# Outputs of two chunks in one transfer of 4 KB rows, in place of one transfer each of 2 KB rows

## The chip, the core and the metric

One core of a Trainium2 chip. The metric is the time of one execution in microseconds on the device. An execution's time is some 1.8 us above the span that its profile shows from the first to the last instruction.

## The reference

Thresholded attention over 8 batches, 8 heads, 576 positions and head size 64, followed by a gated MLP with a mixing over positions. Cut to its shapes and steps:

```python
scores = 0.125 * q @ k.T                     # 8 x 8 x 576 x 576
scores = where(scores >= max - tau, scores, -1e9)
attn   = softmax(scores);  x = attn @ v      # then x as 8 x 576 x 512
h      = relu(x @ w_in)                      # 1024 wide, halves u and v
v_n    = layernorm(v)
v_s    = w_spatial @ v_n + b_spatial         # over the 576 positions
out    = (u * v_s) @ w_out                   # 8 x 576 x 512, float32
```

## The kernel before

The program is one list of 144 steps, some 3 us each. In every step TensorE makes a block of scores, VectorE takes the maximum, ScalarE exponentiates, VectorE (in some steps ScalarE) masks; the probabilities `p` are then transposed by a DMA into `pT`, which TensorE multiplies with `v`. The MLP of a batch is woven in between the attention steps of the next batch and a half: 18 steps make a batch's period. The output of a batch is made in four chunks of 128 rows (`moe_o`, two steps apart) and a remainder of 64 rows. Transfers go out on the queue of SyncE, the engine that here only issues them, in program order, from a list `sends` that each step empties after its transpose.

```python
orr = ctx.enter_context(tc.tile_pool(name="orr", bufs=3))
ptp = ctx.enter_context(tc.tile_pool(name="ptp", bufs=5))      # pT
...
def moe_o(b, c):                       # chunk c of batch b
    def mm():
        t = hold["t"] = bank()         # 4 matmuls into PSUM
        ...
    def ev():
        o = orr.tile([P, 512], F32, name="o") if not wide else stage()
        (nc.scalar.copy if not wide or c % 2 == 0 else nc.vector.tensor_copy)(
            out=o[:n], in_=hold["t"][:n])
        dst = (out[b, 0:512, :].rearrange("(p c) n -> p c n", c=4)[:, c, :] if c < 4
               else out[b, 512:576, :])
        sends.append(lambda: nc.sync.dma_start(out=dst, in_=o[:n]))
...
def mask():                            # the step before's probabilities
    ...
    if c % 2:
        dst = pts[i, c // 2] = ptp.tile([P, 2, 9, P], BF16, name="pT")
        nc.sync.dma_start_transpose(out=dst.rearrange("p c b s -> p (c b) s"),
                                    in_=pt.rearrange("p c s -> p (c s)"))
...
def step(i, c, fs):
    ...
    ready = sends[:]                   # queued by this step and the one before
    sends.clear()
    if unmasked:
        mask()
    for f in ready:
        f()
```

`wide` is empty in the steady part and filled in the tail. Each partition of a chunk holds one row of 2 KB of the output; four chunks of one partition lie side by side in memory, which is why two chunks make rows of 4 KB.

Of the kernel before, what the change touches and what calls it, by code (L numbers as in the profile page):

```python
# [8 lines left out]
F32 = mybir.dt.float32  # L9
# [8 lines left out]
def kernel(  # L18
# [17 lines left out]
    nc = tc.nc  # L36
# [6 lines left out]
    P = 128  # L43
# [7 lines left out]
    xtp = ctx.enter_context(tc.tile_pool(name="xtp", bufs=2))  # L51
    mw = ctx.enter_context(tc.tile_pool(name="mw", bufs=2))
    vr = ctx.enter_context(tc.tile_pool(name="vr", bufs=4))
    orr = ctx.enter_context(tc.tile_pool(name="orr", bufs=3))
    sqr = ctx.enter_context(tc.tile_pool(name="sqr", bufs=1))
    inner = ctx.enter_context(ExitStack())
    ps_f = ctx.enter_context(tc.tile_pool(name="ps_f", bufs=2, space=PSUM))
# [40 lines left out]
    sends = []  # L98
# [118 lines left out]
    wide = []  # L217
    turn = [0]

    def bank(dtype=F32, n=512):  # L220
        if wide:

            turn[0] += 1
            if turn[0] % 8 not in (2, 3):
                return wide[0].tile([P, n], dtype, name="t")
        return ps_f.tile([P, n], dtype, name="f")
# [183 lines left out]
        return "act", mm, ev  # L410

    us, gs = {}, {}
    later = []

    def ends(t, b):
# [112 lines left out]
    def moe_o(b, c):  # L528
        hold = {}
        n = P if c < 4 else 64  # L530

        def mm():
            t = hold["t"] = bank()
            for f in range(4):
                nc.tensor.matmul(out=t[:n], lhsT=gs[b][:, f, c * P:c * P + n],  # L535
                                 rhs=w_o[:, f, :], start=(f == 0), stop=(f == 3))

        def ev():
            o = orr.tile([P, 512], F32, name="o") if not wide else stage()
            (nc.scalar.copy if not wide or c % 2 == 0 else nc.vector.tensor_copy)(  # L540
                out=o[:n], in_=hold["t"][:n])
# [3 lines that stand above are left out]
        return "act", mm, ev  # L545
# [99 lines left out]
    def stage():  # L645

        t = ld_ring[len(staged) // 3 % 2][len(staged) % 3]
        half = len(staged) // 6 % 2
        staged.append(t)
        return t.rearrange("p h c d -> p (h c d)")[:, 512 * half:512 * half + 512]  # L650
# [120 lines left out]
    for b in range(B):  # L771
        n = dict.fromkeys("vuso", 0)
# [132 lines left out]
```

## Time and profile before

| | us |
|---|---|
| median of 3 runs (480.43 to 480.60) | 480.46 |
| the profiled execution | 482.52 |
| its span | 480.7 |

The prediction shows what bounds the kernel. Two more answers belong to it. The first is the view of the tile `o` (line, engine, operation, count: shortest, median and longest in ns, first and last start in us): twenty copies on ScalarE, one for each output that the change touches.

```profile
L540 ACT COPY o<-f x20: 566/585/595, 171.0 to 411.6; 128x512 f32<-128x512 f32 x20
```

The second is the view of who waited for whom (us in total, times, longest): all that TensorE ever waits for a transpose, one place, seen once by the weight load and once by the matmul.

```profile
PEld L289 <- DMA pT<-p: 2.0, 1, 2.0
PE f L289 <- DMA pT<-p: 1.7, 1, 1.7
```

### The profile page before, as it was taken

To read this page: it belongs to the slowest core of one execution; us is meant where nothing else is said; L and a number is where in the kernel's file an instruction comes from. 1 tells how busy PE (TensorE), PEld (TensorE's weight loads), DVE (VectorE), ACT (ScalarE), POOL (GpSimd) and SP (SyncE) were. 2 spreads that over 40 slices of the span, in tenths; PEclk is the share of its full clock that TensorE was granted. 3 is DMA by queue.
4 is the path that set the end of the run, shared out by engine and by line. 5 is a ranking of instruction groups with operands and counts; after the bars stand their busy time and mean duration, and the time that the engine had idled before them with its cause. 6 is when DMAs were issued, how large, how long until landed. Compare 5 with 4: busy or idle time off the path is not lost.

```text
span 480.7 us, 9934 instructions
## 1 busy us (share of the span) xinstructions
PE 449.2 (93%) x3691; PEld 237.4 (49%) x3691; DVE 410.9 (85%) x563; ACT 390.8 (81%) x677; POOL 226.2 (47%) x403
## 2 busy tenths in 40 slices
PE   7788888889999999899999999999999999999995
PEld 4344444444545545354554545445554545445542
DVE  4989888989989997989889888899889998898573
ACT  4789999999879797878978898798978889797251
POOL 3453334794438543555328642375436743253021
PEclk9899999999999999999999999999999999999999
DMA  7979899979988999998989999987998989677523
GB/s 212 265 156 212 184 228 207 188 162 196 187 185 196 168 213 206 179 187 191 199 188 217 177 205 197 217 173 161 212 199 191 207 173 208 144 114 112 149 92 106
DMA packets 227568, 88.49 MB, mean 184 GB/s; under 512 B 197056, under 2 KB 221760, under 8 KB 227520
## 3 DMA queue, kind: packets, MB, share of 16 engines
q1 hardware_dynamic: 226864, 86.98, 86.4%
q8 instruction: 29, 0.48, 0.4%
q0 software_dynamic: 160, 0.52, 0.3%
q10 hardware_dynamic: 496, 0.36, 0.2%
q14 instruction: 19, 0.16, 0.1%
HBM read 33.31 MB, written 9.44 MB: 89 GB/s over the span
## 4 chain that ended last, share of the span: by engine, by line
PE 50%; DVE 20%; ACT 19%; issue 7%; DMA 2%; POOL 0%; POOLq 0%; ACTq 0%
PE s L563 16%; DVE negm L604 9%; DVE p L585 7%; PE s L566 6%; ACT e L621 5%; ACT e L627 5%; PE f L294 4%; PE f L476 4%; PE f L245 3%; PE f L506 2%; PE f L535 2%; ACT vrel L444 2%; PE f L289 2%; DMA pT<-p 2%; ACT p L623 1%
## 5 line engine op out<-in xcount | busy, mean ns | idle before, releaser
L604 DVE TENSOR_REDUCE negm<-s 128x2 f32<-128x1152 f32 x144 | 194.9, 1353 | 35.5 <-PE s L566 35.0
L563 PE MATMUL s<-qkT 64*128 64x512 f32 (+1 forms) x640 | 162.9, 639 | 14.3 <-ACT e L627 8.0
L585 DVE SCALAR_TENSOR_TENSOR p<-e,ctau 128x1152 bf16<-128x1152 f32 x91 | 132.9, 1461 | 1.2 <-ACT e L627 1.1
L627 ACT ACTIVATE e<-s,negm 128x576 f32<-128x576 f32 x182 | 124.7, 740 | 7.8 <-DVE negm L604 7.1
L566 PEld LDWEIGHTS s<-kd,qkT 128*128 128x128 f32 (+1 forms) x320 | 41.5, 178 | 110.7 <-issue 100.1
L621 ACT ACTIVATE e<-s,negm 128x576 f32<-128x576 f32 x106 | 72.8, 740 | 16.9 <-DVE negm L608 11.7
L268 POOL COPY kd<-qkT 64x64 f32<-64x64 f32 x62 | 27.0, 435 | 101.3 <-ACT qkT L263 99.5
L566 PE MATMUL s<-kd,qkT 128*128 128x128 f32 (+1 forms) x320 | 69.9, 322 | 0.0
L563 PEld LDWEIGHTS s<-qkT 64*128 64x128 f32 (+1 forms) x640 | 42.1, 174 | 45.8 <-ACT e L627 17.2
L452 POOL TENSOR_SCALAR nmean<-sm 128x1 f32<-128x1 f32 (+1 forms) x35 | 16.5, 472 | 68.1 <-ACT vrel L444 63.0
L294 PEld LDWEIGHTS <-pT 128*128 128x128 bf16 x1024 | 41.8, 97 | 8.7 <-issue 5.4
L294 PE MATMUL f<-v,pT 128*128 128x65 bf16 x992 | 44.9, 194 | 0.0
L623 ACT ACTIVATE p<-e 128x1152 bf16<-128x1152 f32 x37 | 43.0, 1163 | 1.2
L136 POOL COPY qn<-ql 128x640 f32<-128x640 f32 x31 | 35.0, 1129 | 15.0 <-DMA ql<-in_k_dram 11.0
L289 PE MATMUL f<-v,pT 128*128 128x130 bf16 x124 | 27.2, 219 | 4.7 <-DMA pT<-p 1.7
L464 POOL TENSOR_SCALAR vn<-vrel,rs,nm 128x512 bf16<-128x512 f32 (+1 forms) x34 | 29.6, 872 | 3.7
L506 PE MATMUL f<-wsT,vn 128*128 128x512 bf16 x125 | 31.0, 379 | 0.0
L476 PE MATMUL f<-xT,w_in 128*128 128x512 bf16 x112 | 28.6, 379 | 0.8 <-DVE xn L303 0.7
L434 PE MATMUL f<-w_in,xT 128*128 128x512 bf16 x112 | 28.7, 379 | 0.0
L252 ACT COPY qkT<-f 128x512 f32<-128x512 f32 x31 | 18.2, 588 | 12.8 <-PE f L245 12.8
L303 DVE TENSOR_TENSOR xn<-f,r 128x256 bf16<-128x256 f32 x62 | 26.3, 425 | 2.1
L156 POOL CAST v<-vl 128x640 bf16<-128x640 f32 x32 | 26.4, 824 | 1.6 <-DMA vl<-in_v_dram 1.6
(168 smaller groups left out, 636.8 us busy)
## 6 DMA issues: line engine op xcount, KB each, us to landing
vl<-in_v_dram SPq DMA_DIRECT2D x16, 512.0 KB, 4.6
ql<-in_q_dram SPq DMA_DIRECT2D x15, 512.0 KB, 4.4
kl<-in_k_dram SPq DMA_DIRECT2D x15, 512.0 KB, 4.5
out_dram<-o SPq DMA_DIRECT2D x20, 256.0 KB, 3.4
uT<-in_moe_w_in_dram SPq DMA_DIRECT2D x3, 512.0 KB, 6.2
uT<-in_moe_w_spatial_dram SPq DMA_DIRECT2D x2, 576.0 KB, 5.3
vl<-in_v_dram SPq DMA_DIRECT2D x16, 64.0 KB, 4.2
pT<-p SPq DMA_TRANSPOSE x64, 5.6
```

The source lines that it names most:

```text
L136: nc.gpsimd.tensor_copy(out=t, in_=ld_ring[i // 2 % 2][w][:, 2 * (i % 2):2 * (i % 2) + 2].rearrange("p h c d -> p c h d"))
L289: nc.tensor.matmul(out=t[:, at:at + 130], lhsT=pt[:, 4, :], rhs=vt[:, 4:6, :].rearrange("p b d -> p (b d)"), start=True, stop=False)
L294: nc.tensor.matmul(out=t[:, at + 65 * h:at + 65 * h + 65], lhsT=pt[:, 5 * h + j, :], rhs=vt[:, 6 * h + j, :], start=False, stop=(h == 1 an ...
L476: nc.tensor.matmul(out=t, lhsT=w_in[:, m, f * P:(f + 1) * P], rhs=xts[b][:, m, 0:512], start=(m == 0), stop=(m == 3))
L506: nc.tensor.matmul(out=t, lhsT=vn[:, c, f * P:(f + 1) * P], rhs=wsT[:, c, 0:512], start=(c == 0), stop=(c == 4))
L563: nc.tensor.matmul(out=s[rows, 1024 * h:1024 * h + 512], lhsT=qks[n][hs, 0, m], rhs=qks[n][hs, 1, 0:512], start=True, stop=True)
L566: nc.tensor.matmul(out=view(s[rows], 512, [[448, 2], [1, 64]]), lhsT=qks[n][:, 0, m], rhs=kd_ring[n % 2], start=True, stop=True)
L585: nc.vector.scalar_tensor_tensor(out=pt[:, c % 2, :], in0=ef, scalar=ctau, in1=ef, op0=ALU.is_ge, op1=ALU.mult)
L604: nc.vector.tensor_reduce(out=nm, in_=s, axis=AX.X, op=ALU.max, negate=True)
L621: nc.scalar.activation(out=e[:, h, :], in_=s[:, h, :], func=ACT.Prelu, bias=nm[:, h:h + 1], scale=by, alpha=1e30)
L623: nc.scalar.activation(out=pr_ring[i // 2 % 2] if c == 4 else p_ring[2 * (i % 2) + c // 2][:, c % 2], in_=e.rearrange("p h s -> p (h s)"), ...
L627: nc.scalar.activation(out=e[:, h, :], in_=s[:, h, :], func=ACT.Exp, bias=nm[:, h:h + 1])
```

## The change

Half as many output transfers, each with rows twice as long: less issue time on SyncE and larger packets. The copies stay; the first chunk of a pair waits in the buffer for the second.

```diff
-    orr = ctx.enter_context(tc.tile_pool(name="orr", bufs=3))
+    orr = ctx.enter_context(tc.tile_pool(name="orr", bufs=1))
+    oo = ctx.enter_context(tc.tile_pool(name="oo", bufs=2))
...
+    pair_o = [None]
...
         def ev():
+            if not wide and c < 4:
+                if c % 2 == 0:
+                    pair_o[0] = oo.tile([P, 2, 512], F32, name="oo")
+                o2 = pair_o[0]
+                nc.scalar.copy(out=o2[:, c % 2, :], in_=hold["t"])
+                if c % 2:
+                    rows = out[b, 0:512, :].rearrange("(p c) n -> p c n", c=4)
+                    sends.append(lambda: nc.sync.dma_start(out=rows[:, c - 1:c + 1, :], in_=o2))
+                return
             o = orr.tile([P, 512], F32, name="o") if not wide else stage()
```

## The prediction

> **What bounds the kernel now.** I read the page first: busy shares, then the chain that ended last.
>
> ```profile
> PE 449.2 (93%) x3691; PEld 237.4 (49%) x3691; DVE 410.9 (85%) x563; ACT 390.8 (81%) x677; POOL 226.2 (47%) x403
> ...
> PE 50%; DVE 20%; ACT 19%; issue 7%; DMA 2%; POOL 0%; POOLq 0%; ACTq 0%
> ```
>
> TensorE is busy 93% of the span and half of the chain is on it; DMA is 2% of the chain. So the kernel is bound by TensorE with VectorE and ScalarE close behind, and transfers bound it only where one lands late. Asking the stretches of one batch each (18 steps, 55 us) confirms a steady state; the columns are PE, PEld, DVE, ACT and POOL busy, the clock, the DMA share, and GB/s:
>
> ```profile
> 170.00:225.00 55.00, 52.69 (x439) 27.25 (x437) 48.47 (x62) 45.73 (x80) 25.07 (x47) 1.00 0.93 187
> 225.00:280.00 55.00, 54.40 (x448) 28.41 (x448) 49.13 (x64) 47.34 (x85) 28.11 (x49) 1.00 0.93 195
> ```
>
> In the steady stretch TensorE is busy 54.40 of 55.00 us. In the one before, where the first batch's outputs go out, it is busy 52.69. The DMA engines are at 0.93 in both: not what bounds, but full enough that a queued transfer waits for those ahead of it. Next, the transfers that the change touches, from the DMA view (KB each, median us from issue to landing) and from the view of the output tensor:
>
> ```profile
> out_dram<-o SPq DMA_DIRECT2D x20, 256.0 KB, 3.4
> uT<-in_moe_w_in_dram SPq DMA_DIRECT2D x3, 512.0 KB, 6.2
> ...
> L544 SPq DMA_DIRECT2D out_dram<-o x20: 529/544/587, 179.3 to 414.6; - x20
> ```
>
> Twenty output transfers (four chunks of batches 0 to 4) go out of the small ring in the steady part; those of batches 5 and later leave from other buffers in the tail, and the diff leaves them alone. Each takes 544 ns of SyncE's queue. Nothing is listed as waiting for them. The last thing read was who waits for a DMA at all: in the waits of the whole program TensorE has one place, at 204.68 us, and SyncE's timeline shows what stood ahead of the transfer that it waited for:
>
> ```profile
> 196.50 0.56 SPq L544 DMA_DIRECT2D out_dram<-o  x1
> 197.16 4.24 SPq L589 DMA_TRANSPOSE pT<-p  x1
> ...
> 204.68 0.23 PE L289 MATMUL f<-v,pT 128*128 128x130 bf16 x1 [1.73 <-DMA pT<-p]
> ...
> 252.27 0.56 SPq L544 DMA_DIRECT2D out_dram<-o  x1
> 252.93 4.11 SPq L589 DMA_TRANSPOSE pT<-p  x1
> ...
> 259.98 0.23 PE L289 MATMUL f<-v,pT 128*128 128x130 bf16 x1
> ```
>
> The output of chunk 3 is issued just before the transpose of probabilities that is needed soonest. In batch 0 that transpose took 7.5 us to land and TensorE stood 1.73 us; one batch later it took 6.0 us (DMA view of that stretch), landed at about 258.9, and was used at 259.98, with no wait: a margin of about 1.1 us. I take the same margin for batches 2 to 4, whose steps repeat every 55.2 us.
>
> **What the Trainium skill says.** "DMA: Bandwidth & Descriptors", section "Rules for kernel authors", says to coalesce many small transfers and that under 64 KB one pays mostly overhead. These are 256 KB, so the rule promises little here. [...] a transfer's time is far longer than its issue (3.4 us against 0.544), and nobody waits for these completions, so halving them buys no latency. Section "Queues, rings and completion order" says that each DMA engine takes one ring's descriptors in order. The trace fits: the transpose issued behind 512 KB of loads and 256 KB of output needs 6.0 to 7.5 us against 4.6 for the quickest of all 64. This ordering is what could make the change cost something.
>
> **The change, part by part.**
>
> ScalarE: the 20 copies remain, one each of 128x512 at 583 ns, into halves of a pair tile. Change 0.
>
> SyncE: ten of twenty issues go, 10 x (0.544 + about 0.1 of gap) = 6.4 us of queue time over the program. I take a 4 KB-row issue at the price of a 2 KB-row one, because the 4 KB-row weight loads took 0.43 to 0.59. SyncE is nearly full: adding up the durations of its instructions in 225 to 280 gives 51.5 of 55 us. But it matters only if it starts a needed transpose sooner. In the steady batch (issue slots at 235.11, 239.49, 244.10, 252.27) the slots at 235.11 and 244.10 vanish. The transpose after the first starts at 236.08, while its data comes from VectorE at 234.61 + 1.41 = 236.02: gain 0. The one after the second starts at 244.76, data at 243.21 + 1.41 = 244.62: gain 0.14 us. So in the steady state the issue time is off the path. In batch 0 SyncE runs later: transposes start at 189.51 and 197.16 on data that was ready at 187.52 and 195.28. There both removed slots can move the late transpose earlier, by up to 2 x 0.66 = 1.3 us, unless its queue time is only back-pressure from full DMA engines.
>
> DMA engines: the same 5.2 MB. The packet records of the trace have a median of 84 ns for 2 KB and 159 ns for 4 KB, so 2560 packets of the first, 215 us, become 1280 of the second, 204 us: 11 us over 16 engines, 0.7 us over the whole program and on no path. What moves is the time of chunk 2's 256 KB: from 244.10, eight us ahead of the tight transpose, to 252.27, right ahead of it. Eight more packets of 2 KB on each engine are 8 x 84 ns = 0.67 us. Steady: the margin of 1.1 us falls to about 0.45 + 0.14 = 0.6, still no wait. Batch 0: 1.73 + 0.67 - (0 to 1.3) = 1.1 to 2.4 us, against 1.73.
>
> Ring sizes: three buffers of 2 KB a partition become one of 2 KB and two of 4 KB. The pair ring gives each half at least 12 us after the last copy plus the two-pair alternation, some 40 us in all, against 6 us of queue lag and 3.4 us to land: no wait. The single buffer now serves the four output-weight stages and the remainder rows. The loads at 127.86, 145.60 and 159.63 follow casts that ended at 120.80, 132.62 and 150.97: no wait. The first remainder copy on ScalarE at 166.08 follows the last cast, which ends at 164.22 + 0.61 = 164.83: 1.25 us to spare.
>
> Sum: 480.46 - 0.6 to + 0.7 from batch 0, 0 from the others, 0 from rings. I put the middle at +0.1: 480.6 us.
>
> **The rivals.** First: relief of a nearly full SyncE and of full DMA engines shifts everything forward and the only DMA stall disappears. For it: 93% of SyncE's time is taken and batch 0 lags by 1.9 us. Against: outside batch 0 its transposes start when their data comes. It would give 480.5 - 1.7 = 478.8. Second: the 512 KB burst delays the tight transpose by more than its margin in each of five batches. For it: the 512 KB weight loads landed in 6.2 us, 2.8 more than a 256 KB output, although early and in a crowd; 1.2 us more is what a 512 KB load of values (4.6) costs over an output. With 1.2 us the steady batches stall (1.2 - 1.1 - 0.14, nothing) to, with 2.8, 1.6 us each: 480.5 + 4 x 1.6 + 1 = 488 at the worst, 481.5 when moderate. Third: the buffer ring of one blocks ScalarE behind GpSimd once (the 1.25 us above shrinks if the last weight load is late): up to + 1, once.
>
> **Range and chances.** A stall removed gives 478.8, moderate bursts 481.5 to 482; 2% is 9.6 us, which only the worst burst approaches. Predicted 480.6, range 479.3 to 482.2; faster by over 2% 0.01, within 2% 0.97, slower 0.02.
>
> **What would show it right or wrong.** Right: ten outputs of 512 KB landing near 4 us with an issue near 0.55 us; 20 copies of 583 ns unchanged; the transpose behind the second pair landing about 0.6 us later than now; TensorE waiting for pT only in batch 0, for 1 to 2.4 us; steady TensorE still 54 of 55 us. Wrong: waits of TensorE for pT in several batches (second rival), none at all (first rival), ScalarE's copy of the remainder waiting at 166 us (third), or an issue of a pair that costs as much as two.

## The result, and the profile after

| | median us | runs |
|---|---|---|
| before, same chip | 480.53 | 480.43 to 481.13 (4) |
| changed | 480.66 | 479.22 to 480.89 (4) |

The ratio is 0.9994, with a 95% interval of 0.9973 to 1.0015: the same. Here and below a ratio is the mean time of one kernel's fast runs over that of the other's in the same rounds, so not quite the ratio of the medians quoted.

The profiled execution happened to be the fastest of the four (479.22, span 477.4). Its span is 3.3 us under the profile before, while the medians differ by 0.1 us: comparing the two profiles' totals would invent a gain. Setting the 144 maxima of VectorE side by side in the two traces shows where the 3.3 us lie: 1.5 us are there at 25 us, before any instruction that the change touches, and 1.2 to 1.6 us come between 202 and 211 us, where the execution before waited for `pT`; the rest is in small steps that come and go. The clock shows where most of the first 1.5 us are: in the profile before, TensorE was granted half its clock from 19.84 to 23.25 us, at full work; in the profile after, that stretch is at 1.00. Half of 3.41 us is 1.7.

What the change did do is as intended. The DMA view, and then the view of the tile `oo`, of the changed kernel:

```profile
out_dram<-oo SPq DMA_DIRECT2D x10, 512.0 KB, 3.8
```

```profile
L546 ACT COPY oo<-f x20: 566/586/596, 169.4 to 408.5; 128x512 f32<-128x512 f32 x20
L549 SPq DMA_DIRECT2D out_dram<-oo x10: 372/544/737, 180.2 to 411.5; - x10
```

Ten transfers, at the same 544 ns of queue time each as the 20 before; 3.8 us to land for 512 KB against 3.4 for 256 KB; copies unchanged. The window that answers to the prediction's 252 to 260 us, one batch after the first outputs, is SyncE's timeline of the changed kernel (start, duration in us) and TensorE's first use of the transpose:

```profile
246.75 1.07 SPq L109 DMA_DIRECT2D kl<-in_k_dram  x1
247.88 0.62 SPq L116 DMA_DIRECT2D ql<-in_k_dram  x1
248.59 0.56 SPq L549 DMA_DIRECT2D out_dram<-oo  x1
249.29 4.82 SPq L601 DMA_TRANSPOSE pT<-p  x1
```

```profile
256.89 0.23 PE L290 MATMUL f<-v,pT 128*128 128x130 bf16 x1
```

The transpose is issued 7.60 us ahead of its use, where before it was 7.05 (252.93 to 259.98). The DMA view of this stretch shows when it lands:

```profile
pT<-p SPq DMA_TRANSPOSE x1, 6.8
```

It lands 6.8 us after its issue, where before it took 6.0. So SyncE, rid of one issue, starts the transpose half a microsecond sooner, right when its data is ready (VectorE's masking ends at 249.22), and it takes 0.8 us longer to land behind the 256 KB more. The margin goes from 1.0 to 0.8 us. At this place TensorE waits in neither kernel.

For the argument below I call the four transposes that stand at this place in the batches T0 to T3 (issued near 195, 250, 305 and 361 us). *Lead* is issue to use, *landing* issue to landing, *margin* the difference. The numbers with two digits come from the trace's issue times and DMA completions; where TensorE waits, the lead contains the wait, and the margin reads 0.05, the time from the landing to the matmul.

### The profile page after: what moved, and what is told of

Same layout as the page of the kernel before. It is cut to its first block, busy times and chain, and to the rows that moved or that the text cites. A ratio compares the mean times of both kernels' runs of the same rounds, so it can differ in the third digit from the quotient of the medians.

```text
span 477.4 us, 9856 instructions
## 1 busy us (share of the span) xinstructions
PE 444.8 (93%) x3646; PEld 236.0 (49%) x3691; DVE 409.6 (86%) x563; ACT 390.2 (82%) x677; POOL 227.1 (48%) x403
## 4 chain that ended last, share of the span: by engine, by line
PE 48%; ACT 23%; DVE 21%; issue 7%; POOL 0%; POOLq 0%; ACTq 0%; DVEq 0%
PE s L575 16%; DVE negm L616 9%; DVE p L597 7%; PE s L578 6%; ACT e L633 6%; ACT e L639 5%; PE f L295 4%; PE f L478 3%; PE f L246 3%; ACT p L635 3%; PE f L508 2%; PE f L537 2%; PE f L290 2%; ACT vrel L446 2%; ACT pr L635 2%
## 5 line engine op out<-in xcount | busy, mean ns | idle before, releaser
L575 PE MATMUL s<-qkT 64*128 64x512 f32 (+1 forms) x640 | 161.9, 636 | 15.7 <-ACT e L639 8.3
L478 PE MATMUL f<-xT,w_in 128*128 128x512 bf16 x97 | 27.6, 379 | 1.6 <-DVE xn L304 0.7
L436 PE MATMUL f<-w_in,xT 128*128 128x512 bf16 x102 | 27.4, 379 | 0.3
```

What stands on the lines that cost most here:

```text
L478: nc.tensor.matmul(out=t, lhsT=w_in[:, m, f * P:(f + 1) * P], rhs=xts[b][:, m, 0:512], start=(m == 0), stop=(m == 3))
L575: nc.tensor.matmul(out=s[rows, 1024 * h:1024 * h + 512], lhsT=qks[n][hs, 0, m], rhs=qks[n][hs, 1, 0:512], start=True, stop=True)
```

## Experiments

Kernels are compared only within the same rounds.

| run | what differs | median us | before | ratio (95%) |
|---|---|---|---|---|
| before_again | nothing | 481.19 | 480.26 | 1.0009 (0.9973 to 1.0045) |
| after_again | the change | 480.41 | 480.26 | 0.9992 (0.9967 to 1.0018) |
| none | no output transfers | 480.11 | 480.26 | 1.0004 (0.9965 to 1.0044) |
| quad | one transfer of 8 KB rows | 481.41 | 480.26 | 1.0017 (0.9985 to 1.0049) |
| split4 | 80 transfers of 512 B rows | 493.90 | 480.67 | 1.0285 (1.0238 to 1.0332) |
| split8 | 160 transfers of 256 B rows | 539.68 | 480.67 | 1.1225 (1.1175 to 1.1275) |
| two_together | pairs as two transfers | 480.99 | 480.67 | 1.0007 (0.9978 to 1.0035) |
| deferred | pairs sent two steps later | 479.92 | 480.67 | 0.9982 (0.9957 to 1.0008) |
| split2 | 40 transfers of 1 KB rows | 484.90 | 480.29 | 1.0100 (1.0066 to 1.0133) |
| single_deferred | before, chunk 3 later | 480.07 | 480.29 | 0.9985 (0.9965 to 1.0005) |
| deferred_again | as deferred | 480.62 | 480.29 | 0.9996 (0.9976 to 1.0016) |
| after_third | the change | 480.47 | 480.29 | 0.9995 (0.9976 to 1.0015) |

All runs were correct, except that of `none`, which leaves outputs unwritten.

### The two kernels once more

No edit. The wait in batch 0, on which my working for batch 0 rested, was to be found again or not.

> The kernel before, unchanged, timed against itself and profiled a second time. Theory (the TensorE wait for pT at 205 us is a chance of one execution): ratio 1.000 within 0.15%, span about 478.7, and no wait of 1.7 us for pT in batch 0. Rival (the wait is a property of the schedule of batch 0): the same wait of 1.5 to 2 us again near 205 us, and the pT behind the chunk-3 output landing 7 us or more after its issue.

> The changed kernel, unchanged, profiled a second time and timed in five rounds. Theory (the change is off every path): ratio to before 1.000 within 0.15%; span 478.5 to 479.1; the output pairs land in about 4 us. Rival (relief of the SyncE queue): a repeated span near 477.4 and a ratio of 0.996 or less.

The profiled execution of before_again took 482.89 us, again slower than its median. There is no wait at T0 (landing 5.1 us, margin 2.5). But T2, two batches later, is late in the same way. TensorE's timeline of before_again, and the DMA view of that stretch:

```profile
313.92 0.23 PE L289 MATMUL f<-v,pT 128*128 128x130 bf16 x1 [1.83 <-DMA pT<-p]
```

```profile
out_dram<-o SPq DMA_DIRECT2D x1, 256.0 KB, 4.6
pT<-p SPq DMA_TRANSPOSE x1, 7.6
```

So neither side had it quite: the wait is no property of batch 0, but it is one of this place in the batch. The two late transposes landed 2.3 and 2.1 us later than the same two in the other profile of this kernel, where they had margins of 2.5 and 2.1. In before_again all 16 completions of T2 came between 7.3 and 7.6 us, so it was no single slow DMA engine.

Half of the lateness is SyncE's. From the end of the masking, when the data is ready, to the use there are 7.7 us in the profiles of both kernels (waits left out), so TensorE waits where *lag* (masking to issue) and landing exceed that. In the two late cases the lag was 1.88 and 1.94 us, at the other six places of the two profiles 0.06 to 1.04. In both, another transpose 12 to 14 us earlier had held the queue for longer than the usual 1.2 to 1.3 us, and from there to T0 or T2 SyncE had no gap of much over 0.1 us in which to catch up:

```profile
292.31 2.98 SPq L330 DMA_TRANSPOSE xT<-xn  x1
...
305.63 0.55 SPq L544 DMA_DIRECT2D out_dram<-o  x1
306.29 4.03 SPq L589 DMA_TRANSPOSE pT<-p  x1
```

(before_again; in the profile before it was `ptr`, 2.30 us at 185.14. That this hold made the lag is argued, from two cases; single_deferred below has one of 2.25 us at 293.60 and a lag of 0.06 at T2.) In the three profiles of the changed kernel the lag is 0.06 to 0.57 us. It still had late landings: T2 took 8.2 us in after_again, TensorE waited 0.61 us, and 0.27 us in after_third (landing 7.9). Why a landing takes 7.5 to 8.2 us in one execution and 5.1 to 5.9 in the next, these runs do not show.

Such a wait can cost more than itself. The stretches of 2 us of before_again (columns as in the prediction's table of stretches):

```profile
312.00:314.00 2.00, 0.17 (x4) 0.09 (x3) 1.68 (x3) 1.80 (x5) 1.29 (x4) 1.00 0.84 54
314.00:316.00 2.00, 1.78 (x20) 1.35 (x22) 0.61 (x2) 1.97 (x3) 1.25 (x3) 0.52 0.97 254
316.00:318.00 2.00, 2.00 (x7) 0.59 (x5) 0.73 (x2) 0.39 (x1) 0.00 (x0) 0.63 1.16 215
318.00:320.00 2.00, 2.00 (x12) 1.04 (x10) 2.00 (x2) 0.60 (x1) 0.00 (x0) 1.00 0.67 119
```

The number after the five engines' busy times (1.00, 0.52, 0.63, 1.00) is the mean granted clock. Asked in other stretches, the clock is 0.50 from 314.07 to 317.48 us, 3.41 us long, and 1.00 on both sides. Laid beside the trace of the profile before, which has no wait here, VectorE's maxima lose 3.5 us for a wait of 1.83; the half clock accounts for half of 3.41, 1.7 us. The wait of 1.73 us in the profile before left the clock at 1.00 and cost 1.2 to 1.6. The Trainium skill, "TensorE: Matmul & The Clock Gate", part 1 on the clock gate, says that the array falls to half clock after an idle window of about 3.4 us and needs as long to come back. The recovery time agrees, but the window was not idle: in the 3.41 us up to 314.07 TensorE worked 1.59. Stretches of the same length, counted on from the clock's changes, divide the wait in the profile before between two, with 2.21 and 2.88 us of work. No threshold follows: in split4 below, such a stretch with 1.49 us of work left the clock at 1.00.

### What these transfers can cost at most

```diff
-            sends.append(lambda: nc.sync.dma_start(out=dst, in_=o[:n]))
+            if wide:
+                sends.append(lambda: nc.sync.dma_start(out=dst, in_=o[:n]))
```

> Wrong result on purpose: the twenty output transfers of the steady part are left out, the copies stay. This is the most that any arrangement of these outputs can gain. Theory (they are off the path): ratio 0.997 to 1.001. Rival (SyncE's nearly full queue and the full DMA engines hold the kernel back): 20 issues of 0.66 us and 5.2 MB less give a ratio of 0.99 or less, with the steady period under 55 us.

With all twenty transfers gone the time is the same. The transposes now land in 4.6 to 4.7 us with margins of 2.9 to 3.0 us, and adding up SyncE's instructions between 225 and 280 us gives 44.4 us where the kernel before has 50.3 (counted here only as far as they lie inside the stretch; the 51.5 of the prediction includes whole instructions that cross its edges). So 5.9 us a batch of queue time (2.2 of the four issues, 3.7 of the transposes `pT`, which hold the queue for less time without them) and 5.2 MB of traffic in all can be taken away with nothing to show for it. This is the ceiling of any rearrangement of these outputs, within the noise of 0.4%. Halving the issues could not have gained more than that.

### Double dose

```diff
-                if c % 2 == 0:
-                    pair_o[0] = oo.tile([P, 2, 512], F32, name="oo")
+                if c == 0:                                   # and one buffer in oo
+                    pair_o[0] = oo.tile([P, 4, 512], F32, name="oo")
...
-                if c % 2:
+                if c == 3:
-                    sends.append(lambda: nc.sync.dma_start(out=rows[:, c - 1:c + 1, :], in_=o2))
+                    sends.append(lambda: nc.sync.dma_start(out=rows, in_=o2))
```

> The change at double dose: all four chunks of a batch in one transfer of 8 KB rows, 1 MB, sent with chunk 3, from one buffer. Theory (a burst right ahead of the tight transpose costs its bytes: 8 packets of 4 KB on each engine more than the pair, 8 x 0.159 = 1.3 us): the margin of about 0.8 us in the profile after turns into a wait of about 0.5 us in each of five batches, 2 to 3 us in all, ratio 1.003 to 1.007. Rival (the burst is absorbed): ratio 1.000, no waits for pT. Second rival (fewer issues help): under 0.998.

The DMA view at T1 of quad:

```profile
out_dram<-oo SPq DMA_DIRECT2D x1, 1024.0 KB, 6.8
pT<-p SPq DMA_TRANSPOSE x1, 7.6
```

At T1 the landing rises with what stands ahead: 4.7 us with no output ahead (`none`), 6.0 behind 256 KB, 6.8 behind 512 KB, 7.6 behind 1 MB. The last doubling adds 0.8 us, not the 1.3 that I expected. But these are single profiles: at T2 of quad a transpose behind 1 MB landed in 5.4. The means of T0 to T3 over all profiles of each kernel, 4.7, 6.2, 6.5 and 6.9 us, rise less: 1.5 us for the first 256 KB, then 0.3 and 0.3. The lead stays at 7.6, so the margins are 0.49, 0.05, 2.25 and 0.32 us: used up, but not overdrawn. The summed wait that the profile shows is 0.2 us. The median is 1.0 us over that of the changed kernel, but the ratio's interval holds 1: not shown to be slower.

### The reverse of the change

```diff
-            sends.append(lambda: nc.sync.dma_start(out=dst, in_=o[:n]))
+            k = 1 if wide else 2                             # 4, 8
+            for j in range(k):
+                cs = slice(j * (512 // k), (j + 1) * (512 // k))
+                sends.append(lambda cs=cs: nc.sync.dma_start(out=dst[:, cs], in_=o[:n, cs]))
```

> The kernel before with each output as two transfers of 1 KB rows, 40 issues in place of 20: some 20 x 0.55 = 11 us more queue time, 2.2 us a batch, under the slack that split4 and split8 leave room for (split4 cost 2.6 us a batch of the 6.5 us that it added, so some 4 us a batch were free). Theory: ratio 0.998 to 1.004. Rival (every issue on this queue costs the kernel its time): 1.02 or more.

> The reverse of the change, on the kernel before: each of the twenty outputs sent as four transfers of 512 B rows, 80 issues in place of 20, same bytes. SyncE gets 60 x about 0.65 = 39 us more queue time over five batches, 8 us a batch on a queue that has some 3.5 us a batch free. Theory (SyncE has slack only up to its free time): transposes start late, TensorE waits for pT in every batch, ratio 1.02 to 1.06. Rival (queue time of the transposes is back-pressure and shrinks): ratio under 1.01.

> As split4 with eight transfers of 256 B rows for each output, 160 issues in place of 20: 140 x 0.65 = 91 us more queue time, 18 us a batch. Theory: SyncE is then the bound in these batches, 15 us a batch longer, ratio 1.12 to 1.17. Rival (issues are cheap when the queue is waiting anyway): ratio under 1.05.

Here the queue does set the time. split4's 2.9% is within what I gave, split8's 12.3% too, and split2 is a miss: I had read the free time off split4 as an average of 4 us a batch, and 20 more issues were to cost nothing. They cost 4.6 us. SyncE's timeline of split2, ahead of T1:

```profile
248.94 0.54 SPq L108 DMA_DIRECT2D kl<-in_k_dram  x1
249.53 0.62 SPq L115 DMA_DIRECT2D ql<-in_k_dram  x1
250.25 1.03 SPq L547 DMA_DIRECT2D out_dram<-o  x2
251.38 3.85 SPq L592 DMA_TRANSPOSE pT<-p  x1
```

T1 is used at 257.23, so its lead is 5.85 us, where the kernel before has 7.05: 1.2 us less, about what the two extra issues just ahead, one of chunk 2 and one of chunk 3, take with their gaps. That is more than the margin of 1.0. SyncE's lag behind the data is 0.47, 1.90, 2.39 and 1.78 us at T0 to T3. The margins in split2 are 1.75, 0.05, 0.05 with a wait of 1.97, and 0.49. This profile is the fastest of the six executions (483.15), so it shows the lateness, but not the whole 4.6 us. Free time on a queue cannot be spent where it does not lie: the 4.7 us a batch (55.0 less 50.3) in which SyncE executes nothing in the kernel before lie elsewhere or are the small steps from one instruction to the next, while the queue has no gap of much over 0.1 us in the 17 us before T1. In split4 the leads are 4.6 to 6.1 us, waits included, and TensorE waits at all four:

```profile
PE f L289 <- DMA pT<-p: 10.3, 4, 3.3
```

Those 10.3 us are the larger part of the 13.2 by which its median is longer; two stretches of 3.41 us at half clock, at 206.06 and 322.11, come to at most 3.4 more. Small rows could have slowed the DMA engines instead of the queue, but these four landed in 4.6 to 6.0 us, no slower than before: they were issued late, with lags of 1.82 to 2.71 us. In split8 TensorE waits 24.8 us for `pT` and 15.7 for another transpose, `xT`, by the same view, and its mean clock is 0.951.

### The change without its wide rows

```diff
-                    sends.append(lambda: nc.sync.dma_start(out=rows[:, c - 1:c + 1, :], in_=o2))
+                    for j in range(2):
+                        sends.append(lambda j=j: nc.sync.dma_start(
+                            out=rows[:, c - 1 + j, :], in_=o2[:, j, :]))
```

> The change without its wide rows: pair buffers and the late sending kept, but each pair goes as two transfers of 2 KB rows one behind the other (20 issues again). Theory (neither the row width nor the number of issues is on the path): ratio 0.998 to 1.002, the transpose behind the second pair starts about 0.65 us later after its data than in the changed kernel and lands with 0.2 to 0.6 us less margin. Rival (wide rows are what the DMA engines gain from): clearly slower than the changed kernel, 1.005 or more.

The same time within the noise, so neither row width nor issue count is shown to be on the path. My expectation on margins was not met: they are 1.39, 1.36, 0.05 (a wait of 0.46) and 0.83 us, against 2.22, 0.82, 1.69 and 0.05 in the first profile of the changed kernel. T1's lead is 0.3 us shorter, not 0.65, and it landed sooner, not later. The margins of single profiles scatter by more than the effect that I asked for.

### The second pair behind the transpose

```diff
-                    sends.append(lambda: nc.sync.dma_start(out=rows[:, c - 1:c + 1, :], in_=o2))
+                    later.append((2, lambda: sends.append(lambda: nc.sync.dma_start(
+                        out=rows[:, c - 1:c + 1, :], in_=o2))))
```

> The change with each pair sent two steps later, so that the second pair goes behind the tight transpose and not ahead of it. Theory (the burst ahead of the transpose uses up margin but the margin holds): margin of the transposes that the second pair stood ahead of grows from about 1 us to 2 us, no wait there, and the time stays, ratio 0.997 to 1.001. Rival (the burst costs time in most executions): 0.995 or less.

> The deferred pair once more, unchanged. Theory: ratio 0.997 to 1.000 to before, and again no execution over 481. Rival (the narrow spread in its first rounds was luck): one or more of its executions over 481.5, as before has.

> The changed kernel once more, beside the deferred versions. Theory (its tight transposes have 0.05 to 1.7 us of margin and now and then miss): ratio to before 0.998 to 1.002, median 0.2 to 0.6 us over the deferred version's. Rival: no difference to the deferred version.

And on the kernel before, the chunk-3 output alone:

```diff
+            if c == 3 and not wide:
+                later.append((2, lambda: sends.append(
+                    lambda: nc.sync.dma_start(out=dst, in_=o[:n]))))
+                return
             sends.append(lambda: nc.sync.dma_start(out=dst, in_=o[:n]))
```

> The kernel before, single outputs, with only the chunk-3 output sent two steps later, so that it goes behind the tight transpose. Theory (deferral, not pairing, is what gave the deferred version its steady 479.7 to 480.5): margins of the transposes near 200, 255, 311 and 366 us of about 2 us or more, no late ones among them, median 479.7 to 480.3. Rival (pairing is part of it): no better than before.

SyncE's timeline of deferred now has the transpose ahead of the output:

```profile
248.24 0.63 SPq L116 DMA_DIRECT2D ql<-in_k_dram  x1
249.73 3.60 SPq L602 DMA_TRANSPOSE pT<-p  x1
...
256.04 0.55 SPq L549 DMA_DIRECT2D out_dram<-oo  x1
```

The margins are 1.83, 2.10, 1.97 and 2.42 us, in deferred_again 1.95, 2.88, 1.57 and 2.70, in single_deferred 1.99, 1.58, 1.73 and 1.46. None of these three profiles, nor that of `none`, has a wait of 0.25 us or more at T0 to T3. Of the six profiles in which one or two chunks stand right ahead of the transpose (before twice, the changed kernel three times, two_together), four have one of over 0.4 us, and a fifth one of 0.27. So the order does move the late transposes. That it moves the time is not shown: deferred looked like 0.2% with no execution over 480.5, but its repeat has one of 481.72 and a ratio of 0.9996, and after_third was not slower than it (480.47 against 480.62), both against what I expected. Single_deferred, 479.55 to 480.62, has 0.9985 with 1 inside the interval. No version beats the two kernels by more than the noise.

## Why the prediction was right

The time, 480.66 us, lies 0.06 from the 480.6 predicted, and "within 2%" had 0.97. So small a miss is luck: the kernel before alone has medians of 480.26, 480.67 and 480.29. Point by point:

- **TensorE bounds, transfers only where one lands late.** Right. Taking all twenty transfers away gave 1.0004.
- **Issue time is off the path in the steady state.** Right as a verdict. The size was off: the term "gain 0.14 us" measured 0.3 to 0.55 (leads 7.05 and 7.33 before, 7.60, 7.61 and 7.61 after). I had counted the gain at the transpose before; the last stretch to T1 had more lag to give back.
- **256 KB more ahead of the transpose cost 0.67 us.** Close: T1's landing went from 6.0 and 6.3 us to 6.8, 6.4 and 6.9. Together with the lead this gives margins of 0.82, 1.21 and 0.73 us, where 0.6 was predicted and 1.0 measured before. At T1 the two halves of the change about cancel. Over T0 to T3 the mean landing rises from 6.2 to 6.5 us, half of what was predicted, and the mean lag falls from 0.85 to 0.16; single landings scatter by 2 us and more.
- **Batch 0: "1.73 + 0.67 - (0 to 1.3)".** This step failed. Its premise, a wait that belongs to batch 0, came from one execution, and a second profile of the same kernel does not have it there. The term "0 to 1.3" did name SyncE's lag, which was 1.88 us there; in the changed kernel it is 0.06 at that place, but so it is in before_again without the change. The profile after has no wait of TensorE of 0.25 us or more in any batch, which the prediction had listed as a sign that the first rival holds; it was no such sign, since the time stayed. The warning was in the table: the profiled execution was 2.06 us slower than the median, nearly the wait of 1.73 that it showed (the half clock near 20 us has its part in this). Since I put only + 0.1 us on it, the sum did not suffer.
- **Buffer rings.** Right: the last weight cast of the changed kernel ends at 162.74 + 0.61 = 163.35 us, the remainder's copy starts at 164.53, and the view of the tile `o` lists no wait of ScalarE for GpSimd.
- **First rival (relief moves everything forward, 478.8).** Refuted by `none`, which is more relief than any change of this kind can give.
- **Second rival (the burst overdraws the margin in every batch, 481.5 to 488).** Refuted at this size; quad shows that twice the burst just reaches the margin.
- **Third rival (GpSimd holds ScalarE once).** Did not occur.

What remains open is why a transpose holds the queue or lands late in one execution and not in the next, and whether the deferred order gains the 0.1 to 0.2% that its medians hint at.

## What to carry to other kernels

Before merging transfers, remove them: if the kernel without them takes the same time, nothing about their number or width can help, while making them smaller can still hurt, because a queue in order is as late as the entries just ahead of the one transfer that someone waits for. Count slack at that transfer (from data ready to landing against data ready to use, so that the queue's lag is in it), not as idle time of the queue. And compare the profiled execution's time with the median before building on a wait that it shows.

## What the Trainium skill lacked or had wrong

- "TensorE: Matmul & The Clock Gate", part 1: it gives an idle window of about 3.4 us for the fall to half clock. It does not say how much work a window may hold and still count as idle. Here a stretch of 3.41 us with 1.59 us of TensorE work and a wait of 1.83 was followed by 3.41 us at a clock of 0.50, while a wait of 1.73 us, spread over two such stretches, left it at 1.00, and so did a stretch with 1.49 us of work in split4.
- "DMA: Bandwidth & Descriptors", rules for kernel authors: the advice for many small transfers, "Coalesce into one large transfer", has no word on where in the queue the merged transfer ends up. Here 256, 512 and 1024 KB right ahead of a transpose moved its mean landing from 4.7 us (no output ahead) to 6.2, 6.5 and 6.9.
- "DMA: Bandwidth & Descriptors", on issuing engines: it calls the sequencer's issue time usually small beside the transfer. So it is here (0.544 us against 3.4), but the page does not say what follows for the entries behind. On a queue in order that a transpose shares, 20 more issues of about 0.5 us cost 4.6 us of 480, and 140 more cost 59.
